# Sparse attention and mixture of experts: the scores of a unit in four 64x64 quarters of the array

## The chip, the cores and the metric

One Trainium2 chip, one of its cores. The metric is the device time of one execution in microseconds, taken as the median of several runs; the profile shown is of one further execution. The engines are PE (TensorE, the 128x128 matmul array), DVE (VectorE), ACT (ScalarE), POOL (GpSimd) and SP, which here only issues DMAs.

## The reference

Attention over 8 batches, 8 heads, 576 positions and head width 64, all fp32. The first four heads see a local window, the last four a strided pattern; then every position goes through its best two of eight experts.

```
rel = pos[:, None] - pos[None, :]
mask_local = (rel >= 0) & (rel < 32)
mask_strided = (rel >= 0) & (pos[None, :] % 32 == pos[:, None] % 32)
scores = where(mask, q @ k.T / 8, -1e9);  attn = softmax(scores);  x = attn @ v
logits = x @ w_gate;  noisy = logits + log1p(exp(x @ w_noise)) * noise
top2 experts e of each row, weights softmaxed over the two
out = sum of weight_e * (relu(x @ w1[e]) @ w2[e])
```

Here x has 4608 rows of 512; w1 is 512x1024 and w2 1024x512 for each expert.

## The kernel before, in words

The program has two stages that overlap a little: attention with the routing of each batch, and then the experts.

**Units.** Attention runs over 32 units. A unit is one batch and two heads, either two local or two strided ones, in turn. Its queries are cut into 9 blocks of 64. A local block needs 96 keys (its own 64 and the 32 before), a strided block, whose positions are taken apart by their residue, 72. So a unit has 18 score products, each of 64 queries by 96 or 72 keys with 64 (the head width) summed over: each fills a quarter of the array, 64 rows by 64 columns.

**A unit's steps** (lines as in the profile): SP loads k, q and v (L403). `prep` brings k and q into transposed form kT and qT, head 0 on partitions 0 to 63 and head 1 on 64 to 127: eight of the nine blocks from whole-row tiles (L461, after a reordering copy `ord`, or L471), the ninth, which stands alone in small tiles `k0` and `q0` of 64 partitions, by two transposes (L489). `item` is then called twice a unit, for blocks 0 to 3 and for blocks 4 to 8. An item writes the masks into a PSUM bank with a bf16 product of `twin` (two 64x64 identities side by side, so a 64-row by 128-column product, L518) and adds the products of both heads (L525): head 0 lands on partitions 0 to 63, head 1 on 64 to 127 of the same bank, so the products alternate between the two quarters on the array's diagonal. DVE takes the row maxima of the bank (L536), ACT the exponentials, one instruction per block (L540), PE transposes them (L548), ACT or DVE copies them out as aT, PE multiplies by v (L571, and L577 for the ninth block), DVE divides by the sums (L582 to L595) into xo. `finish` stores xo to x_dram (L612) and transposes it into xT (L634, and L631 for the ninth block of 64 rows); for a strided unit the copy out of PSUM (L247 on ACT or L250 on DVE) also puts the positions back in order, writing every eighth element. After four units `route` runs the gate of a batch (L679), the noisy top two (L682 to L764), and POOL scatters entries into a table (L769).

**Experts.** A job gathers up to 384 rows of one expert (POOL, L905), transposes them (DVE, L930), and multiplies by w1 (L963) and w2 (L1027) in split fp32r products; rows of `out` are read, added to and scattered back. Four jobs use only the entries of the first half of the batches and may run while attention still does. Weights are loaded by SP (L834, L837) into `wraw` and split by ACT and DVE (L839, L840).

**The order.** Nothing in the loop over units sets the order of instructions. Each step is a `Piece` with an engine, a planned duration, a rank and what it reads and writes; `issue_all` lays them out in planned time, lowest rank among those that could start within 120 ns, and that is the order on each engine. Eight PSUM banks are handed out by it; attention keeps to 7 while an expert piece waits. The planner chooses ACT or DVE for copies. SP's DMAs and POOL's stand in one queue each, in planned order, and an instruction waits at the head of its queue.

## Time and profile before

| what | before |
|---|---|
| median of 3 runs (lowest, highest) | 1200.76 us (1199.69, 1200.79) |
| the profiled execution, its own time | 1190.76 us |
| its span, first to last instruction | 1189.0 us |
| mean granted TensorE clock | 0.956 |
| PE / DVE / ACT / POOL busy | 95% / 51% / 33% / 52% |
| last gate of attention starts (L679) | 326.59 us |
| first expert product (L963) | 259.8 us |

The profiled execution took 10.0 us less than the median of the runs. All times inside the program are from it. "PE busy" counts a matmul until its modelled end, so back-to-back small products look busy to the last; the steps from one group's start to the next group's start tell more. The granted clock goes between full speed and half of it. An fp32 product leaves two records on PE, so 8 products are written x16; a transpose leaves one.

### The profile page before, as it was taken

Reading aid. Unit: us, or ns where it says so; the run is one execution under the profiler, and the core shown is the slowest. Engines: PE = TensorE matmul, PEld = TensorE weight load, DVE = VectorE, ACT = ScalarE, POOL = GpSimd, SP = SyncE. Lnnn points to the kernel's source line nnn. Section 1 sums busy time; section 2 is a strip of 40 time slices with the busy share of each in tenths; the row PEclk is TensorE's granted clock in tenths of the full one; section 3 lists DMA queues with packets and bytes.
Section 4 is the critical chain, followed back from the end, with each engine's and each line's share of the span. In section 5 each row is a group of like instructions: output and inputs, shape, how many; then the busy total and the mean of one; then the engine's idle time right before and its main releaser. Section 6 shows DMA issues by size and latency. Waiting matters only on the chain.

```text
span 1189.0 us, 23202 instructions
## 1 busy us (share of the span) xinstructions
...
## 2 busy tenths in 40 slices
...
GB/s 172 173 141 175 195 180 160 138 154 162 231 247 195 231 128 70 134 155 70 131 149 97 140 130 125 159 71 64 146 138 79 78 191 80 75 119 116 83 47 20
DMA packets 211941, 159.01 MB, mean 134 GB/s; under 512 B 90967, under 2 KB 181591, under 8 KB 211808
## 3 DMA queue, kind: packets, MB, share of 16 engines
...
q14 instruction: 53, 0.43, 0.1%
...
## 4 chain that ended last, share of the span: by engine, by line
PE 87%; DMA 4%; DVE 3%; issue 3%; ACT 2%; SPq 0%; another core or an unknown queue 0%; POOL 0%; POOLq 0%; DVEq 0%; ACTq 0%
PE bankA L1027 5%; PE bankG L963 4%; PE bankD L1027 4%; PE bankD L963 4%; PE bankF L1027 4%; PE bankE L963 4%; PE bankC L1027 4%; PE bankG L1027 4%; PE bankB L963 4%; PE bankA L963 4%; PE bankH L963 4%; PE bankC L963 4%; PE bankF L963 4%; PE bankH L1027 4%; PE bankE L1027 4%; PE bankB L1027 3%
## 5 line engine op out<-in xcount | busy, mean ns | idle before, releaser
L905 POOL DMA_INDIRECT xg<-x_dram,gxx x304 | 315.7, 1038 | 180.6 <-issue 76.5
L769 POOL DMA_INDIRECT tab<-ent,addr x96 | 91.7, 955 | 121.0 <-DVE mx L536 24.2
L1057 POOL DMA_INDIRECT out_dram<-prev,tabt x80 | 85.6, 1071 | 94.8 <-issue 38.9
L1004 POOL DMA_INDIRECT prev<-out_dram,gix x80 | 79.6, 995 | 66.4 <-issue 28.6
L930 DVE STREAM_TRANSPOSE xr<-xg 128x512 f32<-128x512 f32 x80 | 84.3, 1054 | 31.5 <-DMA xg<-x_dram,gxx 25.0
L934 ACT CAST xhi<-xr 128x512 fp32r<-128x512 f32 x80 | 47.9, 598 | 86.3 <-DVE xr L930 78.7
L839 ACT CAST w2hi<-wraw 128x512 fp32r<-128x512 f32 x88 | 51.6, 617 | 44.9 <-DMA wraw<-in_moe_w_dram 26.7
L840 DVE TENSOR_TENSOR w1lo<-wraw,w1hi 128x512 fp32r<-128x512 f32 x88 | 60.3, 688 | 11.4 <-ACT w1hi L839 6.3
L936 DVE TENSOR_TENSOR xlo<-xr,xhi 128x512 fp32r<-128x512 f32 x80 | 53.2, 665 | 25.0 <-ACT xhi L934 22.0
L840 DVE TENSOR_TENSOR w2lo<-wraw,w2hi 128x512 fp32r<-128x512 f32 x88 | 57.6, 684 | 5.5 <-ACT w2hi L839 4.0
L839 ACT CAST w1hi<-wraw 128x512 fp32r<-128x512 f32 x88 | 54.2, 618 | 17.6 <-DMA wraw<-in_moe_w_dram 17.3
L982 ACT ACTIVATE hhi<-bankE 128x256 fp32r<-128x256 f32 (+2 forms) x33 | 14.0, 424 | 105.1 <-PE bankE L963 81.8
L963 PE MATMUL bankE<-xhi,w1lo 128*128 128x256 f32 (+3 forms) x132 | 40.0, 303 | 0.4 <-issue 0.4
L963 PE MATMUL bankC<-xhi,w1hi 128*128 128x256 f32 (+3 forms) x128 | 38.3, 299 | 1.9 <-ACT w1hi L839 1.9
L963 PE MATMUL bankE<-xhi,w1hi 128*128 128x256 f32 (+3 forms) x132 | 40.0, 303 | 0.0
L982 ACT ACTIVATE hhi<-bankH 128x256 fp32r<-128x256 f32 (+2 forms) x32 | 13.6, 425 | 79.0 <-PE bankH L963 73.0
L963 PE MATMUL bankD<-xhi,w1hi 128*128 128x256 f32 (+3 forms) x132 | 39.9, 302 | 0.0
L963 PE MATMUL bankD<-xlo,w1hi 128*128 128x256 f32 (+3 forms) x132 | 39.4, 298 | 0.4 <-issue 0.4
L963 PE MATMUL bankE<-xlo,w1hi 128*128 128x256 f32 (+3 forms) x132 | 39.7, 301 | 0.0
L963 PE MATMUL bankD<-xhi,w1lo 128*128 128x256 f32 (+3 forms) x132 | 39.6, 300 | 0.0
L963 PE MATMUL bankG<-xhi,w1hi 128*128 128x256 f32 (+3 forms) x132 | 39.6, 300 | 0.0
L963 PE MATMUL bankG<-xhi,w1lo 128*128 128x256 f32 (+3 forms) x132 | 39.3, 298 | 0.0
...
## 6 DMA issues: line engine op xcount, KB each, us to landing
...
```

What stands on the lines that cost most here:

```text
L769: st = nc.gpsimd.indirect_dma_start(out=tab, out_offset=bass.IndirectOffsetOnAxis(ap=s["addr"].t[:, t, kk:kk + 1], axis=0), in_=s["ent"].t ...
L839: Piece("ACT", act(512) + 30, lambda o: nc.scalar.copy(hi.t, raw.t), rank, read=[raw], alloc=[hi], expert=True)
L840: Piece("DVE", dve(512), lambda o: nc.vector.tensor_tensor(lo.t, raw.t, hi.t.bitcast(F32), ALU.subtract), rank, read=[raw, hi], alloc=[lo] ...
L905: dma(lambda o, i=i, g=g, xg=xg: nc.gpsimd.indirect_dma_start(out=xg.t[:, g, :], out_offset=None, in_=x_dram[:4 * known, :], in_offset=bas ...
L930: Piece("DVE", dve(4 * rows), lambda o, xg=xg, xr=xr, ng=ng, rows=rows: nc.vector.transpose(xr.t[:, :, :rows].rearrange("p c (g i) -> p g ...
L934: Piece("ACT", act(4 * rows), lambda o, xr=xr, rows=rows, cols=cols: nc.scalar.copy(xh.t[:, :, cols], xr.t[:, :, :rows]), rank, read=[xr], ...
L936: Piece("DVE", dve(4 * rows), lambda o, xr=xr, rows=rows, cols=cols: nc.vector.tensor_tensor(xl.t[:, :, cols], xr.t[:, :, :rows], xh.t[:, ...
L963: nc.tensor.matmul(ps.t[:, :width], a.t[:, 128 * d:128 * d + 128], c.t[:, d, :width], start=(m == 0), stop=(m == len(todo) - 1))
L982: Piece("ACT", act(width) + 30, lambda o: nc.scalar.activation(hh.t[:, :width], ps.t[:, :width], AF.Relu), rank, read=[ps], alloc=[hh], ex ...
L1004: dma(lambda o: nc.gpsimd.indirect_dma_start(out=pv.t[:rows, :], out_offset=None, in_=out[:known, :], in_offset=bass.IndirectOffsetOnAxis( ...
L1027: nc.tensor.matmul(ps.t, HT[n, f][p[0]].t[:, cols], W2[n][f][p[1]].t, start=(m == 0), stop=(m == len(todo) - 1))
L1057: st = nc.gpsimd.indirect_dma_start(out=out[:known, :], out_offset=bass.IndirectOffsetOnAxis(ap=tb.t[:rows, i, 0:1], axis=0), in_=pv.t[:ro ...
```

## The change

- `products` replaces the scores of both items: a unit's masks and all 18 products are one piece on PE that takes two banks at once. Bank b belongs to head b, partitions 0 to 63 of it to the even blocks, 64 to 127 to the odd ones; the ninth block of head b stands as a fifth column group on half b. Masks are written by 64x64 products into all four quarters (`twin` and the masks stand on both halves of the partitions for that). The order of the 16 first products goes round the four quarters; the ninth blocks follow as a pair.
- An item is now one head, with both banks' ninth blocks in item 1. The row maximum is taken over five column groups in both items; the exponentials of the ninth block are two instructions of 64 partitions, one from each bank.
- `kq0` holds the ninth block's k on partitions 0 to 63 and its q on 64 to 127 (two DMAs as before), and one 128x128 transpose takes the place of two.
- `finish` transposes the ninth block as full 128 rows (xo's lower half is zero there). For strided units the four transposes write PSUM with a step of eight, so that the copy to xT is contiguous; the stores of x go out in rows of 256 elements where they were of 128. v_0 has 72 partitions, the last 8 zero.
- At the start DVE makes two copies of masks and five more memsets.

```diff
-    twin = consts.tile([QB, 2, QB], BF16, name="twin")
-    for h in range(2):
-        nc.vector.tensor_copy(twin[:, h, :], ident[:QB, :QB])
...
+    halves = [slice(QB * h, QB * h + QB) for h in range(2)]
+    twin = consts.tile([2 * QB, QB], BF16, name="twin")
+    for r in halves:
+        nc.vector.tensor_copy(twin[r, :], ident[r, r])
...
+            if o.psums:
+                n = len(o.psums)
                 if o.expert and left_a and held[0] >= expert_banks:
                     return None
-                if not free or not o.expert and e == "PE" and filler[0] and len(BANKS) - len(free) - held[0] >= ATT_BANKS:
+                if len(free) < n or not o.expert and e == "PE" and filler[0] and (
+                        len(BANKS) - len(free) - held[0] + n - 1 >= ATT_BANKS):
                     return None
-                t = max(t, min(free.values()) + 220)
+                t = max(t, sorted(free.values())[n - 1] + 220)
...
-            ("k0", [QB, 2, D], F32, 2), ("q0", [QB, 2, D], F32, 2),
+            ("kq0", [2 * QB, 2, D], F32, 2),
...
+        put("kq0", R["kq0"].new(),
+            [(lambda t, r=r: t[r], src, base + (512 * D if local else 0), [[D, QB], [S * D, 2], [1, D]], 65536)
+             for r, src in zip(halves, (k, q))], True)
...
             ps = Slot()
-            ks, qs = L["k0"], L["q0"]
-            def tr(o):
-                for i, s in enumerate((ks, qs)):
-                    nc.tensor.transpose(ps.t[:, QB * i:QB * i + QB], s.t, ident[:QB, :QB])
-            Piece("PE", 120, tr, rank, read=[ks, qs], psum=ps)
+            kq = L["kq0"]
+            Piece("PE", 115, lambda o: nc.tensor.transpose(ps.t[:, :2 * QB], kq.t, ident), rank, read=[kq], psum=ps)
...
-    def item(u, i, kT, qT, L, xo, rank):
+    def products(u, kT, qT, rank):
...
+        local = units[u][2]
+        w = KW if local else G
+        sc = [Slot(), Slot()]
+        def scores(o):
+            sv = [s.t[:, :5 * w].rearrange("r (n c) -> r n c", n=5) for s in sc]
+            for half in range(2):
+                for b, r in enumerate(halves):
+                    if local:
+                        spans = [(0, 5, mask_l2[r, 1:2, :])] if half else [(0, 1, mask_l2[r, 0:1, :]),
+                                                                           (1, 5, mask_l2[r, 1:2, :])]
+                    else:
+                        spans = [(0, 4, mask_s2[r, 0:1, :]), (4, 5, mask_s2[r, 1:2, :])]
+                    for n0, n1, mk in spans:
+                        nc.tensor.matmul(sv[b][halves[half], n0:n1, :], twin[r, :], mk.to_broadcast([QB, n1 - n0, w]),
+                                         start=(n0 == 0), stop=False, skip_group_check=True)
+            def product(b, s, half, blk):
+                r = halves[b]
+                rhs = kT.t[r, QB * blk:QB * blk + KW] if local else kT.t[r, blk, :]
+                nc.tensor.matmul(sv[b][halves[half], s, :], qT.t[r, blk, :], rhs, start=False,
+                                 stop=True, skip_group_check=True)
+            for s in range(4):
+                for half in range(2):
+                    for b in range(2):
+                        product(b, s, half, 2 * s + half)
+            for b in range(2):
+                product(b, 4, b, NBL - 1)
+        o = Piece("PE", 20 + 10 * w / 4.8 + 5 * (188 if local else 144), scores, rank, read=[kT, qT], psum=sc)
+        o.order += in_turn[-1:]
+        in_turn.append(o)
+        return sc
...
-        sc, mx, ex = Slot(), R["mx"].new(), R["ex"].new()
+        sc, mx, ex = scs[i], R["mx"].new(), R["ex"].new()
         aT, rs = R["aT"].new(), R["rs"].new()
-        def scores(o):
-            sv = sc.t[:, :nb * w].rearrange("r (n c) -> r n c", n=nb)
-            if local:
-                spans = [(0, nb, mask_l[:, 1:2, :])] if i else [(0, 1, mask_l[:, 0:1, :]), (1, nb, mask_l[:, 1:2, :])]
-            else:
-                spans = [(0, 4, mask_s[:, 0:1, :])] + ([(4, nb, mask_s[:, 1:2, :])] if i else [])
-            for n0, n1, mk in spans:
-                nc.tensor.matmul(sv[:, n0:n1, :], twin.rearrange("p h x -> p (h x)"),
-                                 mk.to_broadcast([QB, n1 - n0, w]), start=(n0 == 0), stop=False, skip_group_check=True)
-            for n in range(nb):
-                blk = 4 * i + n
-                rhs = kT.t[:, QB * blk:QB * blk + KW] if local else kT.t[:, blk, :]
-                for h in range(2):
-                    r = slice(64 * h, 64 * h + 64)
-                    nc.tensor.matmul(sv[r, n, :], qT.t[r, blk, :], rhs[r], start=False, stop=True,
-                                     skip_group_check=True)
-        o = Piece("PE", 110 + nb * w / 2.4 + (188 if local else 144) * nb, scores, rank, read=[kT, qT], psum=sc)
-        o.order += in_turn[-1:]
-        in_turn.append(o)
...
-        Piece("DVE", dve(nb * w), lambda o: nc.vector.tensor_reduce(mx.t[:, :nb], view(sc), AX.X, ALU.max, negate=True),
+        Piece("DVE", dve(5 * w), lambda o: nc.vector.tensor_reduce(mx.t, view(sc), AX.X, ALU.max, negate=True),
               rank, read=[sc], alloc=[mx])
         def exps(o):
-            for n in range(nb):
+            for n in range(4):
                 nc.scalar.activation(exv()[:, n, :], view(sc)[:, n, :], AF.Exp, bias=mx.t[:, n:n + 1])
-        Piece("ACT", nb * (act(w) + 82), exps, rank, read=[sc, mx], alloc=[ex])
+            for r, s, m in zip(halves, scs, mxs) if i else ():
+                nc.scalar.activation(exv()[r, 4, :], view(s)[r, 4, :], AF.Exp, bias=m.t[r, 4:5])
+        Piece("ACT", (4 + 2 * i) * (act(w) + 82), exps, rank, read=[*scs, *mxs] if i else [sc, mx], alloc=[ex])
...
         def scaled(o):
-            dst = xo.t[:, 2 * i:2 * i + 2, :, :].rearrange("r g h d -> r (g h) d") if local else xo.t[:, :4, i, :]
-            nc.vector.tensor_tensor(dst, main()[:, :, :D], rs.t[:, :4, None].to_broadcast([128, 4, D]), ALU.mult)
-            if i:
+            if local:
+                nc.vector.tensor_tensor(xo.t[:, :4, i, :], main()[:, :, :D], rs.t[:, :4, None].to_broadcast([128, 4, D]),
+                                        ALU.mult)
+            else:
+                nc.vector.tensor_tensor(
+                    xo.t[:, i:4:2, :, :].rearrange("r m h d -> r h m d"),
+                    main()[:, :, :D].rearrange("r (h m) d -> r h m d", h=2),
+                    rs.t[:, :4].rearrange("r (h m) -> r h m", h=2)[:, :, :, None].to_broadcast([128, 2, 2, D]), ALU.mult)
+            if nb > 4:
                 nc.vector.tensor_tensor(xo.t[:QB, 4, :, :], extra()[:, :, :D],
                                         rs.t[:QB, 4:, None].to_broadcast([QB, 2, D]), ALU.mult)
-        Piece("DVE", 80 * (1 + i), sums, rank, read=[po], alloc=[rs])
-        Piece("DVE", 95 * (1 + i), recip, rank, write=[rs], read=[rs])
-        Piece("DVE", dve(256) + i * dve(128), scaled, rank, read=[po, rs],
+        Piece("DVE", 80 * (nb - 3), sums, rank, read=[po], alloc=[rs])
+        Piece("DVE", 95 * (nb - 3), recip, rank, write=[rs], read=[rs])
+        Piece("DVE", dve(256) + (nb - 4) * dve(128), scaled, rank, read=[po, rs],
...
         else:
             for half in range(2):
-                store(lambda t, half=half: t[64 * half:64 * half + 64, :4, :, :].rearrange("r g h d -> r g (h d)"),
-                      (QB + half) * 128, [[NJ * 128, QB], [2 * 128, 4], [1, 128]], 131072)
+                store(lambda t, half=half: t[64 * half:64 * half + 64, :4, :, :].rearrange(
+                    "r (m g) h d -> r m (g h d)", m=2),
+                      (QB + 2 * half) * 128, [[NJ * 128, QB], [4 * 128, 2], [1, 256]], 131072)
             store(lambda t: t[:QB, 4, :, :].rearrange("r h d -> r (h d)"), 0, [[128, QB], [1, 128]], 32768)
...
             def tr(o, c=c, ps=ps):
                 if c:
-                    nc.tensor.transpose(ps.t[:, :QB], xo.t[:QB, 4, :, :], ident[:QB, :QB])
+                    nc.tensor.transpose(ps.t[:, :128], xo.t[:, 4, :, :], ident)
                 else:
+                    pv = ps.t.rearrange("r (x m h g) -> r m g h x", m=2, h=2, g=2)
                     for g in range(4):
-                        nc.tensor.transpose(ps.t[:, 128 * g:128 * g + 128], xo.t[:, g, :, :], ident)
-            Piece("PE", 60 if c else 430, tr, rank, read=[xo], psum=ps)
+                        nc.tensor.transpose(ps.t[:, 128 * g:128 * g + 128] if local else pv[:, g // 2, g % 2, :, :],
+                                            xo.t[:, g, :, :], ident)
+            Piece("PE", 110 if c else 430, tr, rank, read=[xo], psum=ps)
             def dst(c=c):
                 if local:
                     return xt.t[:, 512:] if c else xt.t[:, :512]
-                return xt.t[:, :QB] if c else xt.t[:, QB:].rearrange("r (x j) -> r j x", j=NJ)
+                return xt.t[:, :QB] if c else xt.t[:, QB:]
             def src(ps=ps, c=c):
                 if c:
                     return ps.t[:, :QB]
-                return ps.t if local else ps.t.rearrange("r (j x) -> r j x", j=NJ)
+                return ps.t
             Piece("ANY", {"ACT": act(n), "DVE": dve(n)}, lambda o, dst=dst, src=src: copy(o.e, dst(), src()), rank,
```

**Where it moves instructions.** PE, the scores of the first local unit, before (twin is the pair of identities, kT_l and qT_l the transposed k and q):

```order
L518 LDWEIGHTS twin
L518 MATMUL bankE<-mask_l,twin 128x96
L518 LDWEIGHTS twin
L518 MATMUL bankE<-mask_l,twin 128x288
L525 MATMUL bankE<-kT_l,qT_l 64x96 x8
L518 LDWEIGHTS twin
L518 MATMUL bankC<-mask_l,twin 128x480
L525 MATMUL bankC<-kT_l,qT_l 64x96 x10
```

and in the changed kernel, with the same products in turn on two banks:

```order
L532 MATMUL bankG<-mask_l,twin 64x96
...
L532 MATMUL bankG<-mask_l,twin 64x384
...
L532 MATMUL bankA<-mask_l,twin 64x96
...
L532 MATMUL bankA<-mask_l,twin 64x384
...
L532 MATMUL bankG<-mask_l,twin 64x480
...
L532 MATMUL bankA<-mask_l,twin 64x480
L538 MATMUL bankG<-kT_l,qT_l 64x96
L538 MATMUL bankA<-kT_l,qT_l 64x96
```

Three mask products a unit became six (three became eight in a strided unit), and one piece stands where two stood with other work between them.

SP, the first loads, before:

```order
L403 DMA ks<-in_k_dram 72x2x512
L403 DMA k_185<-in_k_dram 64x2x64
L403 DMA qs<-in_q_dram 72x2x512
L403 DMA q_189<-in_q_dram 64x2x64
L403 DMA v_s_123<-in_v_dram 72x8x64
```

and now:

```order
L417 DMA ks<-in_k_dram 72x2x512
L417 DMA qs<-in_q_dram 72x2x512
L417 DMA kq_197<-in_k_dram 64x2x64
L417 DMA v_s_125<-in_v_dram 72x8x64
L417 DMA v_127<-in_v_dram 64x2x64
L417 DMA kq_197<-in_q_dram 64x2x64
```

The number of loads is the same; the second half of the small tile moved behind a load of v.

PE, around the last gate (L679, now L716), before. 96 products of layer 1 and 12 of layer 2 of the experts stand ahead of that gate; L1027 is layer 2, L686 and L730 belong to the routing of the last batch:

```order
L1027 MATMUL bankG<-w2hi,hlo 128x512
L679 MATMUL bankC<-xT,wg 32x192 x12
L1027 MATMUL bankD<-w2hi,hhi 128x512
...
L686 MATMUL bankE<-ident,lgT 96x96 x2
L1027 MATMUL bankG<-w2hi,hhi 128x512
...
L730 MATMUL bankH<-ohs,upper 96x48
```

and now, with 96 and 42 ahead of it (L1064 is layer 2, L1000 layer 1, L723 and L767 the routing):

```order
L716 MATMUL bankB<-xT,wg 32x192 x12
L1064 MATMUL bankG<-w2hi,hhi 128x512
...
L723 MATMUL bankA<-ident,lgT 96x96 x2
L1000 MATMUL bankE<-xhi,w1hi 128x256
...
L767 MATMUL bankH<-ohs,upper 96x48
```

So 30 products of layer 2 moved ahead of the last gate; between the gate and L767 stand 6 products of layer 2 and 24 of the next job's layer 1, where 12 of layer 2 stood.

81 lines of the change are left out of this document (41 added, 40 removed).

## The prediction

> **What bounds the kernel now.** I read the chain of waits first, then the span cut into three stretches, then PE step by step. Chain by engine, and the stretches (length, then busy us and instructions of PE, weight loads, DVE, ACT and POOL, then granted clock, DMA share, GB/s):
>
> ```profile
> PE 87%; DMA 4%; DVE 3%; issue 3%; ACT 2%; SPq 0%; another core or an unknown queue 0%; POOL 0%; POOLq 0%; DVEq 0%; ACTq 0%
> 0.00:327.00 327.00, 299.33 (x3665) 234.27 (x3668) 192.74 (x786) 162.45 (x549) 118.12 (x241) 0.88 0.74 171
> 327.00:430.00 103.00, 93.86 (x542) 79.86 (x537) 67.29 (x141) 44.18 (x91) 65.47 (x78) 0.95 0.76 220
> 430.00:1189.00 759.00, 739.48 (x4251) 663.68 (x4249) 348.75 (x615) 189.00 (x403) 431.86 (x464) 0.99 0.36 106
> ```
>
> The change touches the first stretch, attention: PE is busy 299 of 327 us there, DVE 193, ACT 162, so PE's steps come first. Two things dilute them. The DMA engines are at 0.74 on the mean, and the clock at 0.88 means about 78 us at half speed (0.12 x 327 / 0.5). Three short stretches show both (same columns):
>
> ```profile
> 66.00:68.00 2.00, 0.64 (x5) 0.43 (x3) 0.69 (x1) 1.35 (x6) 1.00 (x2) 0.50 0.94 223
> 70.00:80.00 10.00, 10.00 (x88) 7.44 (x86) 4.18 (x14) 1.88 (x6) 3.01 (x6) 0.50 0.66 138
> 130.00:140.00 10.00, 9.55 (x143) 7.60 (x141) 7.61 (x49) 7.28 (x24) 1.88 (x5) 1.00 0.95 229
> ```
>
> From 70 to 80 PE never rests and still goes at half speed. From 130 on the DMA engines are full; of the 33 ten-us stretches to 330 eight have a share of 0.90 or more.
>
> **The scores, now.** PE at full clock (start, busy us, line, operation, count; the step is the time to the next row's start):
>
> ```profile
> 42.20 0.27 PE L489 MATMUL bankD<-ident,k 64*128 64x64 f32 x1
> ...
> 42.47 0.66 PE L461 MATMUL bankB<-ident,ord 128*128 128x128 f32 x4
> 43.05 0.69 PE L571 MATMUL bankH<-v_l,aT 96*64 96x65 f32 x16
> ...
> 43.90 0.29 PE L518 MATMUL bankG<-mask_s,twin 64*128 64x288 bf16 x1
> 44.12 0.72 PE L525 MATMUL bankG<-kT_s,qT_s 64*64 64x72 f32 x16
> 44.77 0.33 PE L518 MATMUL bankC<-mask_s,twin 64*128 64x288 bf16 x2
> 45.03 0.84 PE L525 MATMUL bankC<-kT_s,qT_s 64*64 64x72 f32 x20
> 45.80 0.66 PE L634 MATMUL bankA<-ident,xo 128*128 128x128 f32 x4
> 46.39 0.27 PE L631 MATMUL bankF<-ident,xo 64*128 64x64 f32 x1
> 46.59 0.65 PE L461 MATMUL bankE<-ident,ord 128*128 128x128 f32 x4
> 47.08 0.60 PE L548 MATMUL bankB<-ident,ex 128*72 128x128 f32 x4
> 47.61 1.50 PE L679 MATMUL bankH<-xT,wg 128*32 128x192 f32 x24
> 49.04 0.69 PE L571 MATMUL bankG<-v_s,aT 72*64 72x65 f32 x16
> ...
> 50.31 0.27 PE L548 MATMUL bankE<-ident,ex 128*72 128x128 f32 x1
> 50.51 0.34 PE L518 MATMUL bankC<-mask_l,twin 64*128 64x96 bf16 x2
> 50.78 0.88 PE L525 MATMUL bankC<-kT_l,qT_l 64*64 64x96 f32 x16
> 51.59 0.69 PE L571 MATMUL bankD<-v_s,aT 72*64 72x65 f32 x16
> ...
> 52.58 0.37 PE L518 MATMUL bankB<-mask_l,twin 64*128 64x480 bf16 x1
> 52.88 1.04 PE L525 MATMUL bankB<-kT_l,qT_l 64*64 64x96 f32 x20
> 53.85 0.53 PE L548 MATMUL bankH<-ident,ex 128*96 128x128 f32 x3
> ```
>
> Strided: masks 0.22 + 0.26, products 0.65 + 0.77, together 1.90 a unit. Local: masks 0.27 + 0.30, products 0.81 + 0.97, together 2.35. Ten products take 0.16 more than eight (local) and 0.12 (strided): that is one pair on the diagonal, and 0.81 - 4 x 0.16 leaves 0.17 fixed a group. The 288-column mask (0.22) and the 480-column one (0.30) give 0.10 fixed and 0.42 ns a column.
>
> **The scores, after.** If four quarters go at once, 18 products are four steps of four and one pair: local 5 x 0.16 + 0.17 = 0.97 for 1.78, strided 5 x 0.12 + 0.17 = 0.77 for 1.42. No row has 64x64 products in four quarters. The nearest that share the array are the three column tiles of L679: 24 records of 192 columns in 1.43 us, 0.31 ns a column, where the diagonal pair takes 0.16 / (4 x 96) = 0.42. So three at a time get further than two. At L679's rate a step of four would take 0.24 and 0.18, and the sum below would be 15 instead of 24; I take full overlap, because three tiles already reach nine tenths of their share (0.28 by the pair's rate).
>
> The masks lose the shared write of both halves. If all quarters overlap they cost what one long mask does (0.30 and 0.26), if none 4 x 0.20 + 0.10 = 0.90 and 4 x 0.15 + 0.10 = 0.70. They start in program order. In a strided unit the 72-column mask waits for the 288-column one of its own quarter, and the next quarter's waits behind it: 4 x 0.12 + 0.03 + 0.10 = 0.61. A local unit puts the short mask first, so the last long one starts about 0.10 after the first: 0.40. I take these.
>
> Per unit: local -0.81 - 0.17 = -0.98, strided -0.65 + 0.13 = -0.52; times 16 each, **-24.0 us** at full clock. Ends: all overlaps, -1.08 and -0.87, 31 us less; only diagonals overlap, as now, and masks not at all: -0.17 + 0.33 and -0.17 + 0.22 (one fixed part fewer), 3.4 us more.
>
> **The other PE edits.** Two transposes of k and q (L489, 0.27) become one like the single L548 (0.20): 32 x -0.07 = -2.2. The ninth block's finish goes from 0.20 (L631) to that same 0.20: 0. The four strided transposes of finish will write PSUM with a step of eight elements. L461 already writes with a step of four, in 0.58 and 0.49, where L634 writes contiguously in 0.59: I take 0. PE sum: **-26 us**.
>
> **ACT, DVE, SP.** (start, busy, line, forms; a tile's copies with lowest, median and highest ns; waits at SP's head with total, times, longest.)
>
> ```profile
> 64.19 0.96 ACT L540 ACTIVATE ex<-bankC,mx 128x72 f32<-128x72 f32 x4 [4.37 <-DVE mx L536]
> 65.11 1.21 ACT L540 ACTIVATE ex<-bankA,mx 128x72 f32<-128x72 f32 x5
> 63.65 0.44 DVE L536 TENSOR_REDUCE mx<-bankC 128x4 f32<-128x288 f32 x1
> 64.02 0.52 DVE L536 TENSOR_REDUCE mx<-bankA 128x5 f32<-128x360 f32 x1
> L250 DVE COPY xT<-bankG x4: 1084/1090/1103, 39.4 to 275.7; 128x512 f32<-128x512 f32 x4
> L250 DVE COPY xT<-bankA x4: 194/686/694, 46.5 to 324.9; 128x512 f32<-128x512 f32 x3, 128x64 f32<-128x64 f32 x1
> 6.57 0.46 DVE L250 COPY kT_s<-bankB 128x288 f32<-128x288 f32 x1 [2.61 <-PE bankB L471]
> L612 SPq DMA_DIRECT2D x_dram<-xo x80: 377/570/3094, 21.7 to 323.8; - x80
> SPq L612 <- DVE xo L595: 24.4, 11, 6.7
> ```
>
> One more exponential a unit, 0.25 x 32 = +8.0; a longer maximum, 0.08 x 32 = +2.6; 16 copies of xT at 1.09 become contiguous ones at 0.69, -6.4. That is +4.2 over two engines with 130 and 160 us free: 0, and 4 if none of it were covered. The new DVE work at the start (two mask copies, five memsets, about 1 us) lies in DVE's idle 2.61 before 6.57; uncovered, 1. On SP half of the small k/q tile moved behind two loads of v: at about 0.57 an issue its transpose is 1.1 late in the first unit. Later units load ahead, and the transpose is the last of its unit's: 0, ends 0 and 1.1 a unit, 35. Stores get half as many, longer rows, the same bytes: 0, with 2 us of gain as the other end.
>
> The new wait: a head's maximum now stands behind all 18 products. DVE's queue holds the copies behind it, and ACT's exponentials wait for it as at 64.19 (4.37). It comes about 0.5 later for the first item and sooner for the second; values follow 4.9 us after scores (44.12 to 49.04), which covers it. That the scores want two free banks at once has no row; ends are 0 and one exponential group (1.0) a unit, 32. The plan starts scores where two are free, so I take 0 for it and let the next part hold the rest.
>
> **How much reaches the end.** Not all 26. A quarter of the stage (8 of 33 stretches) has full DMA engines, where PE only waits longer. In about another quarter SP's loads queue behind stores that wait for a unit's end (24.4 us, eleven times, up to 6.7; that they hold a quarter is my estimate). Ends none and all; I take half, **13 us**. Of it 7.0 appear as expert work: 30 products of layer 2 now ahead of the last gate, at 0.233 (six from 339.06 to 340.46). The gate itself comes about 6 earlier, 320.6. Behind it:
>
> ```profile
> ACT w1hi L839 <- DMA wraw<-in_moe_w_dram: 15.4, 13, 3.3
> 334.17 0.22 PE L730 MATMUL bankH<-ohs,upper 96*96 96x48 bf16 x1 [2.88 <-DVE oh L715]
> 339.06 0.40 PE L1027 MATMUL bankD<-w2hi,hhi 128*128 128x512 f32 x1
> ...
> 340.46 0.40 PE L1027 MATMUL bankG<-w2hi,hhi 128*128 128x512 f32 x1
> ```
>
> ACT waits here for weights that come when they come, 1.2 us a time. The fillers after the gate are now layer-1 products of the next job and need them. Two such waits more, 2.5 us, are lost (ends: -2.9, the gap before L730 filled, and 15). 13 - 2.5 = 10.5: the profiled execution's 1190.76 becomes 1180.3. It ran 10.0 below the median, so 1200.76 becomes **1190.3**; with a third or two thirds of the 26 instead of half, 1184 to 1197 after rounding outward.
>
> **Rivals.** *All of it arrives* (0.17): PE 299 of 327 busy speaks for it, the full DMA stretches against. 26 less 2: 1177. *The loads set the stage* (0.12): DMA 0.74 and SP's waits speak for it, that PE is 87% of the chain against. PE's gain becomes waiting: 1200. *Slower by the clock* (0.10): denser scores leave PE lighter between units, and more spells run at half speed. For it: about 78 us run so now, and at 66 to 68 such a spell holds a PE that works 0.64 of 2.00; against it, 70 to 80, where full work stays slow. Each us more at half clock costs half of one, so it decides from 21 us more; with half as much again, 39, it costs 20 against 10.5: 1210. [...] *Writes with a step of eight slow the transposes* (0.03): if the 16 groups double, 16 x 0.59 = 9.4 comes back, the PE sum is 17, half of it less 2.5 is 6: 1195. The step grows from four to eight; that L461 is not slowed by four speaks against. [...] *Quarters on the same rows take turns* (0.03): the change then doesn't do what it says, and PE has 3.4 - 2.2 more: 1202.
>
> **How the numbers follow.** Forecast 0.55, rivals as given. I call 0.2% (2.4 us) what a measurement can tell from no change. Faster: 0.55 + 0.17 + 0.03 = 0.75. Within: the loads' case 0.12 and two thirds of the last, 0.14. Slower: the clock and the rest, 0.11. The range from 1176 to 1204 takes in the forecast, the first two rivals and the last; the clock's case (0.10) is left out, and as much again for the tails of the others.
>
> **What would show it.** Each unit's scores, masks first to next group, at 1.4 local and 1.4 strided at full clock (2.4 and 1.9 if quarters take turns); xT copies all near 0.69; finish's strided transposes at 0.59, not 1.2; the last gate near 320 with 42 products of layer 2 ahead; half-clock time near 78 us; DMA share of attention up to about 0.76. A gate at 327 with PE less busy would mean the loads; half-clock time over 100, the clock; ACT waiting over 5 us more for weights, that the gain was given back after the gate.

## The result: faster, by three times the forecast

| | before | changed |
|---|---|---|
| median of 4 runs (lowest, highest), us | 1200.22 (1197.92, 1200.79) | 1165.51 (1158.95, 1166.78) |
| ratio, 95% interval | | 0.971 (0.967 to 0.974) |
| profiled execution, its span | 1190.76, 1189.0 | 1158.95, 1157.1 |
| last gate starts | 326.6 | 300.7 |
| from there to the end of the span | 862.4 | 856.4 |

The forecast was 1190.3 with a range down to 1176; the change gained 34.7 us and lies below the range. In the profiled executions the spans differ by 31.9: 25.9 ahead of the last gate, although 30 more products of layer 2 (7.0 us) stand ahead of it, and 6.0 behind it. One slow execution of the change in e7_after_again took 4219 us and is left out of the median given for that run below.

The span of the changed kernel in three stretches (columns as in the prediction), with the cut at the gate:

```profile
0.00:303.00 303.00, 257.07 (x3806) 207.91 (x3806) 195.07 (x796) 170.15 (x594) 123.35 (x242) 0.92 0.82 191
303.00:400.00 97.00, 88.02 (x509) 77.85 (x509) 61.93 (x134) 41.54 (x86) 65.44 (x80) 0.93 0.75 217
400.00:1157.00 757.00, 736.97 (x4234) 660.36 (x4232) 346.47 (x613) 188.17 (x401) 421.67 (x463) 0.99 0.35 106
```

PE is busy 257 us of attention where it was 299, and idle 46 where it was 28. The clock is 0.92 instead of 0.88, about 50 us at half speed instead of 78. DMA share went from 0.74 to 0.82: much the same bytes (by the GB/s 56 and 58 MB) in less time.

PE's steps in the changed kernel, at full clock: a strided unit's scores (L532 masks, L538 products), what follows them, and a local unit's scores.

```profile
39.46 0.31 PE L532 MATMUL bankG<-mask_s,twin 64*64 64x288 bf16 x1
39.47 0.31 PE L532 MATMUL bankB<-mask_s,twin 64*64 64x288 bf16 x1
...
39.60 0.19 PE L532 MATMUL bankG<-mask_s,twin 64*64 64x72 bf16 x1
...
39.64 0.25 PE L538 MATMUL bankG<-kT_s,qT_s 64*64 64x72 f32 x1
...
40.40 0.69 PE L598 MATMUL bankD<-v_l,aT 96*64 96x65 f32 x16
...
41.73 0.27 PE L500 MATMUL bankF<-ident,kq 128*128 128x128 f32 x1
41.84 0.60 PE L579 MATMUL bankA<-ident,ex 128*72 128x128 f32 x4
...
54.00 0.23 PE L532 MATMUL bankA<-mask_l,twin 64*64 64x96 bf16 x1
...
54.01 0.39 PE L532 MATMUL bankA<-mask_l,twin 64*64 64x480 bf16 x1
...
54.06 0.32 PE L532 MATMUL bankA<-mask_l,twin 64*64 64x384 bf16 x1
...
54.23 0.24 PE L538 MATMUL bankA<-kT_l,qT_l 64*64 64x96 f32 x1
...
55.16 0.37 PE L723 MATMUL bankE<-ident,lgT 96*96 96x96 f32 x2
55.46 0.69 PE L598 MATMUL bankD<-v_s,aT 72*64 72x65 f32 x16
55.97 0.40 PE L603 MATMUL bankD<-v,aT 72*64 72x65 f32 x4
56.30 0.47 PE L485 MATMUL bankC<-ident,qs 72*128 72x72 f32 x4
```

| step at full clock, us | before | forecast | measured |
|---|---|---|---|
| local: masks, products | 0.57, 1.78 | 0.40, 0.97 | 0.23, 0.93 |
| strided: masks, products | 0.48, 1.42 | 0.61, 0.77 | 0.18, 0.76 |
| ninth blocks of k and q | 0.27 | 0.20 | 0.11 |
| strided values, second item | 0.99 | (not seen) | 0.84 |

The order of the starts is the news: all four 288-column masks start within 0.02 us, and the 72-column ones from 39.60 on, though in the program each stands right behind the 288-column mask of its own quarter and ahead of the next quarter's. In the local unit a 480-column mask starts at 54.01 and the 384-column ones, which stand ahead of it, at 54.06.

Sums: scores 16 x (1.19 + 0.96) = 34.4, ninth transposes 32 x 0.16 = 5.1, strided values 16 x 0.15 = 2.4, together 41.9 us less of PE at full clock, where 26 were forecast. The budget up to the gate: 41.9 less of PE and some 9 from 28 us less at half clock (the 9 is a difference, not a measurement), less 18 more of idle PE, is the 25.9 and the 7.0.

Two corrections to the description. In a strided unit partitions 0 to 63 and 64 to 127 of kT and qT hold the even and odd positions, not the two heads (the ninth block alone is by head). An item of the changed kernel is therefore one head in a local unit and one parity in a strided one; no number hangs on that. And the change also brings a new rule of the planner, which the description leaves out and the forecast doesn't name:

```diff
             for s in write:
                 self.order.append(s.writers[0])
+
+                for x in read:
+                    if s.ring is not None and x.ring is None and x not in s.writers[0].touch:
+                        x.writers[0].order.append(s.writers[0])
```

A piece that fills a PSUM bank for a tile already begun is now planned no earlier than the first copy into that tile. It stands in all versions of the change, in e1_rest, g2_rest and h2_ninth below, and not in h1_xt.

### The profile page after: what moved, and what is told of

The parts are those of the page before. It is cut to its first block, busy times and chain, and to the rows that moved or that the text cites. A ratio compares the mean times of both kernels' runs of the same rounds, so it can differ in the third digit from the quotient of the medians.

```text
span 1157.1 us, 23398 instructions
## 1 busy us (share of the span) xinstructions
PE 1082.1 (94%) x8546; PEld 946.1 (82%) x8546; DVE 603.5 (52%) x1542; ACT 399.9 (35%) x1081; POOL 610.5 (53%) x783
## 4 chain that ended last, share of the span: by engine, by line
PE 85%; issue 3%; DMA 3%; DVE 3%; ACT 2%; another core or an unknown queue 0%; SPq 0%; POOL 0%; POOLq 0%; DVEq 0%; ACTq 0%
PE bankH L1064 5%; PE bankA L1064 5%; PE bankB L1000 5%; PE bankF L1000 5%; PE bankB L1064 4%; PE bankF L1064 4%; PE bankA L1000 4%; PE bankE L1000 4%; PE bankG L1000 4%; PE bankD L1000 4%; PE bankC L1000 4%; PE bankH L1000 4%; PE bankC L1064 4%; PE bankE L1064 4%; PE bankD L1064 4%; PE bankG L1064 4%
## 5 line engine op out<-in xcount | busy, mean ns | idle before, releaser
L942 POOL DMA_INDIRECT xg<-x_dram,gxx x304 | 308.5, 1015 | 180.1 <-issue 85.5
L806 POOL DMA_INDIRECT tab<-ent,addr x96 | 94.5, 985 | 95.4 <-issue 14.8
L1019 ACT ACTIVATE hhi<-bankD 128x256 fp32r<-128x256 f32 (+2 forms) x31 | 13.2, 426 | 88.6 <-PE bankD L1000 65.0
L1000 PE MATMUL bankB<-xhi,w1hi 128*128 128x256 f32 (+3 forms) x132 | 40.2, 305 | 1.5 <-ACT hhi L1019 1.3
L1000 PE MATMUL bankE<-xhi,w1hi 128*128 128x256 f32 (+3 forms) x136 | 41.2, 303 | 0.3 <-issue 0.3
L1000 PE MATMUL bankB<-xhi,w1lo 128*128 128x256 f32 (+3 forms) x132 | 40.1, 304 | 0.8 <-issue 0.7
L1000 PE MATMUL bankE<-xhi,w1lo 128*128 128x256 f32 (+3 forms) x136 | 40.5, 298 | 0.0
L1000 PE MATMUL bankF<-xhi,w1lo 128*128 128x256 f32 (+3 forms) x128 | 39.1, 305 | 1.5 <-DVE w1lo L877 1.5
L1000 PE MATMUL bankE<-xlo,w1hi 128*128 128x256 f32 (+3 forms) x136 | 40.2, 296 | 0.0
L1000 PE MATMUL bankB<-xlo,w1hi 128*128 128x256 f32 (+3 forms) x132 | 39.7, 301 | 0.4 <-issue 0.4
L1000 PE MATMUL bankC<-xhi,w1hi 128*128 128x256 f32 (+3 forms) x132 | 39.4, 299 | 0.0
L1000 PE MATMUL bankF<-xhi,w1hi 128*128 128x256 f32 (+3 forms) x128 | 39.1, 305 | 0.3 <-issue 0.3
L1000 PE MATMUL bankC<-xhi,w1lo 128*128 128x256 f32 (+3 forms) x132 | 39.3, 298 | 0.0
```

Source lines behind the costliest of these rows:

```text
L806: st = nc.gpsimd.indirect_dma_start(out=tab, out_offset=bass.IndirectOffsetOnAxis(ap=s["addr"].t[:, t, kk:kk + 1], axis=0), in_=s["ent"].t ...
L942: dma(lambda o, i=i, g=g, xg=xg: nc.gpsimd.indirect_dma_start(out=xg.t[:, g, :], out_offset=None, in_=x_dram[:4 * known, :], in_offset=bas ...
L1000: nc.tensor.matmul(ps.t[:, :width], a.t[:, 128 * d:128 * d + 128], c.t[:, d, :width], start=(m == 0), stop=(m == len(todo) - 1))
L1019: Piece("ACT", act(width) + 30, lambda o: nc.scalar.activation(hh.t[:, :width], ps.t[:, :width], AF.Relu), rank, read=[ps], alloc=[hh], ex ...
```

## The experiments

All ratios are to the kernel before, timed in turn on the same chip. The change is called "the change", and "us" in a comparison is worked out from medians.

| run | what | ratio (95% interval) | kernel before on that chip |
|---|---|---|---|
| e6_before_again | before | 0.999 (0.995 to 1.003) | 1159.5 |
| e7_after_again | change | 0.986 (0.977 to 0.995) | 1159.5 |
| f1_after | change | 0.988 (0.983 to 0.992) | 1161.3 |
| e8_after | change | 0.972 (0.968 to 0.977) | 1200.7 |
| e3_by_quarter | change, products by quarter | 0.998 (0.994 to 1.002) | 1160.0 |
| f2_by_quarter | the same | 0.995 (0.992 to 0.998) | 1161.3 |
| g1_by_quarter | the same | 0.985 (0.980 to 0.991) | 1195.0 |
| e4_twice | change, scores twice | 0.998 (0.995 to 1.002) | 1160.0 |
| f3_twice | the same | 0.994 (0.991 to 0.997) | 1161.3 |
| e1_rest | all but the quarters | 0.994 (0.990 to 0.997) | 1160.0 |
| g2_rest | the same | 0.984 (0.979 to 0.989) | 1195.0 |
| h1_xt | contiguous xT alone | 0.999 (0.996 to 1.003) | 1199.1 |
| h2_ninth | ninth-block edits, planner's new rule | 0.982 (0.977 to 0.987) | 1199.1 |
| e5_old_cost | change, old plan costs | 0.999 (0.994 to 1.003) | 1160.0 |
| e9_fill | change, PE filled | 0.975 (0.969 to 0.981) | 1200.7 |
| e10_no_v | change, few loads of v | 0.973 (0.967 to 0.979) | 1200.7 |
| e11_store_act | change, stores by ACT | 0.992 (0.989 to 0.995) | 1200.7 |
| f4_two_ks | change, two k tiles | 0.987 (0.983 to 0.991) | 1161.3 |

### Two kinds of chips

The first four runs were meant to split the change into its parts.

e1_rest is the kernel before with everything but the quarters and what hangs on them (an item per head, the longer rows of the stores):

```diff
-            ("k0", [QB, 2, D], F32, 2), ("q0", [QB, 2, D], F32, 2),
+            ("kq0", [2 * QB, 2, D], F32, 2),
...
-                    kw = w if local else QB
-                    nc.tensor.matmul(extra()[:, h, :], aT.t[:kw, 4, 64 * h:64 * h + 64], rhs, start=True, stop=True)
+                    nc.tensor.matmul(extra()[:, h, :], aT.t[:w, 4, 64 * h:64 * h + 64], rhs, start=True, stop=True)
...
-                    nc.tensor.transpose(ps.t[:, :QB], xo.t[:QB, 4, :, :], ident[:QB, :QB])
+                    nc.tensor.transpose(ps.t[:, :128], xo.t[:, 4, :, :], ident)
...
-                        nc.tensor.transpose(ps.t[:, 128 * g:128 * g + 128], xo.t[:, g, :, :], ident)
+                        nc.tensor.transpose(ps.t[:, 128 * g:128 * g + 128] if local else pv[:, g, :, :],
+                                            xo.t[:, g, :, :], ident)
```

> The kernel before with every part of the change except the four quarters: one transpose for the ninth blocks of k and q, ninth value products over 72 rows, full-row finish, contiguous copies of xT. Theory A (the quarters carry nearly all of the 35 us, the rest only its 5 to 7 us of PE steps): 1193 to 1198. Rival B (the rest carries a good part, because copies, stores and fewer switches of row count free other engines too): 1185 or less.

Measured: 1152.3, and the kernel before beside it took 1160.0 at the median of 31, not 1200. So the times that these first expectations name can't be compared; ratios can, and by its ratio of 0.994 the run lies in theory A's bounds (0.993 to 0.998). Two runs asked whether this was the chip:

> The kernel before, unchanged, as a run of its own with a profile, on the chip of this call. In the runs so far on another chip the kernel before took 1160 at the median of 31, where it had taken 1200 when the change was timed. Theory A (chips differ in the pace of loads or in the clock, and where attention is not held back by PE the change has less to give): the time is again well under 1200, the ratio to the kernel before is 1.00 by construction, and the trace shows a last gate some 25 us earlier than 326.6 with less half-clock time or higher GB/s. Rival B (the 1160 came from something in that one call): 1195 to 1202 with the last gate at 327.

> The changed kernel, unchanged, on the same chip as the run of the kernel before. Theory A (the gain depends on the chip's state: where the kernel before takes 1160, the change gains 0 to 10): 1150 to 1160, ratio 0.99 to 1.00. Rival B (the change gains its 3% everywhere, and the four kernels of the last call were all slowed by what they undo): ratio 0.97, 1125 beside 1160 or 1165 beside 1200.

Before 1161.2 and change 1146.9, on another chip again; a third gave 1161.3 and 1147.0, a fourth 1200.7 and 1167.0:

> The changed kernel on the chip of this call, the base for the three other runs here. So far two kinds of chips were met: the kernel before took 1200 and the change 1165 to 1167 on the one, 1160 and 1148 on the other. Theory A: one of these two pairs again. Rival B: a ratio of 0.97 also where the kernel before takes 1160, which would make the run with 1148 a stray.

> The changed kernel once more, beside the kernel before on one chip, to place the earlier runs. Theory (the gain is set by how much half-clock time the kernel before meets on the chip of the day: per batch of four units the traces so far give 33.6 us plus 0.54 for each us at half clock before, 30.7 plus 0.58 after): with 1160 before, 1146 to 1152, ratio 0.988 to 0.994; with 1200 before, 1160 to 1167. Rival (the gain is the same 3% on every chip): ratio 0.968 to 0.974.

The last gate of the kernel before came at 308.1 in e6, 18.5 earlier than in the first profile, with 58 instead of 78 us at half speed before it. That is theory A of e6, with a smaller shift than its 25. The change's 0.986 in e7 is just outside A's 0.99 to 1.00 (its interval reaches 0.995), f1 repeats one of the two known pairs, and the same 3% on every chip is out (f1: 0.983 to 0.992). The times of e8 and f1 fall within e8's theory, 1167.0 at its very edge; that half-speed time sets the gain, as that theory has it, isn't shown by this.

So there are two kinds of chips for this kernel. On the one (call it the 1200 kind: the first timing and three chips of the experiments) the change gains 34 to 35 us, on the other (the 1160 kind, three chips) 13 to 14.

What tells the kinds apart in the trace is not the length of any common instruction (their medians agree within 2% in e8 and f1) and not the transfers (591 and 588 us of work for each DMA engine there), but the waits that the profile puts down to "issue", in which an engine waits for nothing that is seen. In the dense part (430 to 1130 us) of the change on a chip of the 1200 kind, groups by waiting instruction (total us, times, longest):

```profile
POOL xg L942 <- issue: 68.6, 180, 3.8
DVE hlo L1024 <- issue: 38.8, 31, 3.1
ACT hhi L1019 <- issue: 26.9, 19, 7.1
```

and of the same kernel on a chip of the 1160 kind, where DVE and ACT have no such row:

```profile
POOL xg L942 <- issue: 46.5, 140, 4.5
POOL out_dram L1094 <- issue: 28.0, 31, 14.0
```

In attention (0 to 300 us) PE has 36 such waits (14.0 us in all) on the first and none on the second. Over all runs the DVE row parts the kinds (39 us and more against 2 and less), while PE's waits do so less cleanly (5.4 us and more against 6.8 and less). The clock differs as well: the kernel before was granted 0.955 at the median on two chips of the 1200 kind (about 108 us at half speed) and 0.969 on the 1160 kind (72 us), while the change was granted 0.960 and 0.958, nearly the same. Why a chip is of one kind was not tried.

### The quarters

Undone by order alone: the 18 products go quarter after quarter, all other instructions stay.

```diff
-            for s in range(4):
-                for half in range(2):
-                    for b in range(2):
-                        product(b, s, half, 2 * s + half)
-            for b in range(2):
-                product(b, 4, b, NBL - 1)
+            for b in range(2):
+                for half in range(2):
+                    for s in range(4):
+                        product(b, s, half, 2 * s + half)
+                    if b == half:
+                        product(b, 4, b, NBL - 1)
```

> The changed kernel with the 18 products of a unit written quarter after quarter (4 or 5 in a row into the same quarter) instead of in turn; everything else in the same order. The trace of the change shows masks of a later quarter starting before the second mask of an earlier one. Theory A (each quarter has its own line of waiting products, and order in the program matters little): 1164 to 1170, score steps of about 1.2 local and 0.95 strided. Rival B (PE starts products in program order, so only the ends of quarters overlap): a local unit's products take up to 18 x 0.16 = 2.9 instead of 0.9, 2.0 more, strided 1.5 more, 56 us of PE in all, and two thirds of that at the end: 1195 to 1210.

PE by steps, a local unit of f2_by_quarter:

```profile
54.62 0.23 PE L532 MATMUL bankA<-mask_l,twin 64*64 64x96 bf16 x1
...
54.85 1.12 PE L538 MATMUL bankA<-kT_l,qT_l 64*64 64x96 f32 x15
55.74 0.29 PE L538 MATMUL bankH<-kT_l,qT_l 64*64 64x96 f32 x1
55.82 0.24 PE L538 MATMUL bankA<-kT_l,qT_l 64*64 64x96 f32 x1
55.87 0.24 PE L538 MATMUL bankH<-kT_l,qT_l 64*64 64x96 f32 x1
55.90 0.24 PE L538 MATMUL bankA<-kT_l,qT_l 64*64 64x96 f32 x1
55.96 0.24 PE L538 MATMUL bankH<-kT_l,qT_l 64*64 64x96 f32 x1
55.98 0.24 PE L538 MATMUL bankA<-kT_l,qT_l 64*64 64x96 f32 x1
56.04 1.12 PE L538 MATMUL bankH<-kT_l,qT_l 64*64 64x96 f32 x15
57.09 0.37 PE L723 MATMUL bankE<-ident,lgT 96*96 96x96 f32 x2
```

The unit takes 2.47, in rival B's direction though less, with the masks as quick as ever (0.23). A quarter alone takes 0.16 a product, and the next quarter does wait while several products of the one ahead stand in a row. The rows show how long: the first product into bankH starts at 55.74, when three records into bankA (55.82, 55.90, 55.98) have yet to start; a product is two records. It is three at this place in all 79 units of the three runs by quarter that ran at full clock without a break. The masks fit that: when the last 288-column mask starts, three 72-column ones that stand ahead of it are still waiting. So three blocked records were passed in both cases. The step went up by 1.31 local and, at 1.97, by 1.03 strided: 37.4 us of PE. And yet the time moved little on this chip; hence the repeat beside the change on one chip, with a second way to add PE work:

> The changed kernel with products written quarter after quarter, which by its trace costs 2.47 instead of 1.16 a local unit and 1.97 instead of 0.94 a strided one: 16 x 2.34 = 37 us more of PE steps at full clock, nothing else changed, now on the same chip as the change. Theory A (about 0.6 of PE's steps reach the end): +18 to +28 against the change. Theory B (waits for other engines and loads set the stage): under +8. Theory C (all of it counts): +34 or more.

The other way computes masks and products twice:

```diff
-        o = Piece("PE", 20 + 10 * w / 4.8 + 5 * (188 if local else 144), scores, rank, read=[kT, qT], psum=sc)
+        o = Piece("PE", 20 + 10 * w / 4.8 + 5 * (188 if local else 144), lambda o: (scores(o), scores(o))[1], rank, read=[kT, qT], psum=sc)
```

> The changed kernel with masks and products of every unit computed twice in a row, the second time over the first; same order on all engines. It adds 16 x (1.16 + 0.94) = 34 us of PE steps at full clock. Theory A (PE sets the pace of attention, about two thirds of its work counts): +20 to +30, 1186 to 1196. Rival B (loads set the pace and the gain came from elsewhere): under +8, below 1174. Rival C (PE counts in full, and slower score steps bring back half-clock time): +34 or more, 1200 and above.

> The changed kernel with masks and products computed twice, by its trace 2.19 instead of 1.16 local and 1.75 instead of 0.94 strided: 16 x 1.84 = 29 us more of PE steps, on the same chip as the change. It differs from the run by quarters in that the array is in full use meanwhile. Theory A (0.6 of PE's steps, the clock follows use of the array, and half-clock time comes out lower than by quarters): +8 to +18, and at least 5 less than by quarters. Theory B (only steps count): four fifths of what the run by quarters costs.

Change 1147.0, by quarter 1154.9, twice 1154.0: 37.4 us of PE cost 7.9, and 29 cost 7.0, on the 1160 kind, each within some 5 us by the scatter of the runs. (On the chip of e3 and e4 the change itself wasn't timed; if it has its 0.986 to 0.988 there, their 0.998 means some 12 to 14.) Where the rest of the 37.4 stays is seen in attention up to the gate, which starts at 294.25 in the change and 302.68 by quarter; first row the change (f1_after), second by quarter:

```profile
0.00:294.00 294.00, 247.50 (x3782) 204.55 (x3782) 194.75 (x795) 170.53 (x594) 124.03 (x242) 0.88 0.83 194
0.00:303.00 303.00, 280.71 (x3788) 241.02 (x3791) 201.18 (x796) 172.09 (x594) 124.02 (x242) 0.92 0.81 189
```

PE is idle 46.5 us in the change and 22.3 by quarter: 24 of the 37 that the change saves only turned into waiting. And the clock is 0.88 against 0.92, about 70 us at half speed against 48: here the PE with less to do was granted less clock, worth about 5 by difference. What is left, 8.4, is the gate. Theories A and C of f2 are out, and B (under 8) is met at its edge. For f3, A is out; whether 7.0 is B's four fifths of 7.9 is beyond the scatter. A's part on the clock holds weakly: 0.972 granted at the median for the scores done twice, 0.9685 by quarter, 0.9575 for the change.

On the 1200 kind:

> The run by quarters once more (37 us more of PE steps than the change, all else the same), for a chip of the kind where the kernel before takes 1200 and the change 1166. On the other kind it cost 8 us. Theory A (there the saved PE steps reach the end, because the same chips show waits of all engines for their own instructions, and these lie on the path together with PE): 1186 to 1205, 20 us or more over the change. Theory B (the difference between the kinds of chips lies outside the scores): 1170 to 1178. On a chip where the kernel before takes 1160: 1153 to 1160, as before.

1178.65 beside 1195.0: 0.985, where the change has 0.972 and 0.971 on that kind. The quarters are worth 1.3%, some 15 us of their 37 (7 to 24 by the intervals), compared through the kernel before across chips; that is between theory A and theory B. Attention up to the gate, which starts at 322.8, 18 later than in e8_after:

```profile
0.00:323.00 323.00, 293.04 (x3788) 250.32 (x3791) 197.50 (x795) 172.09 (x594) 123.03 (x242) 0.90 0.76 177
```

PE is idle 30 us here and 45 in e8, so less of the work hides in waits than on the 1160 kind. The clock is 0.90 in both: in these two traces the busier PE was not granted more (0.965 against 0.9605 at the median of the runs).

### The rest

> The kernel before with all parts of the change but the quarters, for a chip of the kind where the kernel before takes 1200. On the other kind it gained 8 us of the 13. Theory A (quarters carry most of the gain where it is 34): 1185 to 1196. Theory B (the rest carries most of it, as on the other kind): 1180 or less. On a chip where the kernel before takes 1160: 1149 to 1156.

1172.9 beside 1195.0: the rest alone gives 1.6% (1.1 to 2.1) on the 1200 kind, 0.6% (0.3 to 1.0) on the 1160 kind. By quarter, the other way to take the quarters out, gave 0.985 and 0.995, so the two agree. The rest carries about half of the gain, against the forecast's 2.2 of 26; g2's time is in theory B's bounds. Its two parts were timed apart: h1_xt has only finish's strided writes and the contiguous copies, h2_ninth only the one transpose of k and q, value products over 72 rows and the full-row finish (the first three pieces of the diff above), and with them the planner's new rule, which h1_xt doesn't have.

> The kernel before with one part of the rest alone: finish's strided transposes write PSUM with a step, so that the 16 copies of xT are contiguous (1.09 to about 0.69 us each on DVE or ACT; no PE step changes). The whole rest gave 22 us where the kernel before took 1195 and 8 us where it took 1160. Theory A (DVE and ACT lie on the chain from scores to the end of a unit, so shorter copies count): a third to two thirds of the rest, 7 to 14 us or 3 to 5 us by the kind of chip. Theory B (the copies are hidden, as the prediction had it): within 2.4 us.

> The kernel before with the other part of the rest alone: one transpose for the ninth blocks of k and q, ninth value products over 72 rows, full-row finish of the ninth block. By steps in the traces 0.15 us less a unit for the transpose and 0.15 less a strided unit for the values, 7.3 us of PE in all, with no more work elsewhere. Theory A (PE steps count by half or more): 4 to 8 us less than before on either kind of chip. Theory B (the order that the plan makes of new durations moves more than the steps): outside that, on either side.

The copies did become short (two banks' groups of h1_xt, ns lowest, median, highest), and the time didn't move:

```profile
L250 DVE COPY xT<-bankG x4: 691/692/693, 39.7 to 282.3; 128x512 f32<-128x512 f32 x4
L250 DVE COPY xT<-bankD x4: 677/686/692, 93.1 to 305.6; 128x512 f32<-128x512 f32 x4
```

They were hidden, as forecast (0.996 to 1.003). The ninth-block edits with the planner's rule give 1.8% (1.3 to 2.3), about 19 us, where the PE steps are 7.5 us shorter. Theory A's 4 to 8 fell, and theory B's "outside that" is met. Two further differences are known. The plan for h2_ninth puts 36 products of layer 2 ahead of the last gate instead of 12 (24 x 0.233 = 5.6 us of expert work done in waits). And its granted clock was 0.9645 at the median against 0.955 for the kernel before on the same chip, some 24 us less at half speed; among the runs of one kernel a us at half speed goes with 0.2 to 0.4 of time in most cases, so 5 to 10. Together with the steps that is enough for 19, but the three were not taken apart, no run has the edits without the rule or the rule without the edits, and that new plan and clock are the cause stays argued, not shown.

### What holds attention after the change

With PE idle 46 of 300 us, four runs looked for the next limit.

```diff
                 def tr(o):
+                    for _ in range(4 if (which, c) == ("k", 0) else 0):
+                        nc.tensor.matmul(ps.t.rearrange("r (a x) -> r a x", a=2), warm[:, :128],
+                                         warm[:, None, :].to_broadcast([128, 2, 256]), start=True, stop=True)
```

> The changed kernel with four bf16 products of 128x128 by 512 columns, of zeros, put ahead of the first transposes of k of every strided unit, where PE waits for a load (about 0.85 us each time at full clock, 14 us in all). They are free where PE waits there anyway. Theory A (half-clock time costs about half of itself, and is brought on by PE's light load at such waits): half-clock time of attention falls by 20 us or more, and the time by 0 to 8 us. Theory B (loads set the floor, the clock follows other things): half-clock time stays within 10 us, time 0 to +5. Rival C (PE's work counts in full): +14.

Attention of e9_fill, and of the change on the same chip:

```profile
0.00:304.00 304.00, 260.73 (x3846) 207.75 (x3846) 195.07 (x796) 170.86 (x594) 122.76 (x241) 0.95 0.82 188
0.00:304.00 304.00, 258.67 (x3780) 210.16 (x3781) 193.65 (x794) 169.31 (x592) 122.29 (x241) 0.90 0.80 186
```

Half speed fell from about 60 to 30 us, as theory A says: here the clock rose with more work on PE (0.971 against 0.9605 at the median of the runs). The time did not fall with it: the last gates start at 304.2 and 304.8, and the medians are 1168.2 and 1167.0. That the filling took what the clock gave is the likely reading.

```diff
-            put("v", slot, parts, True)
+            put("v", slot, parts if u < 4 else parts[:1], True)
...
-                 for h in range(2)], True)
+                 for h in range(2)] if u < 4 else
+                [(lambda t: t[:, 0, :1, :D], v, base, [[NJ * D, G], [D, 1], [1, D]], 18432)], True)
```

> The changed kernel without most loads of v: from the fifth unit on a unit loads only a first small piece of v and multiplies by the v of earlier units, so its output is not the reference's. It leaves out some 10 MB of the 36 MB that the units load. Theory A (after the change the loads set the floor of 30.7 us a batch): a batch falls to 27 us or less at full clock, 15 to 30 us less in all. Theory B (PE and the chain from load to store still set it): under 8 us less.

```profile
0.00:301.00 301.00, 260.84 (x3787) 212.79 (x3788) 197.81 (x809) 177.71 (x598) 122.18 (x240) 0.90 0.66 163
```

DMA share 0.66 instead of 0.80, and the same time (1168.0): the gate came 3.4 earlier than in e8, and the stretch behind it took 4.8 longer. The DMA engines' capacity isn't the limit on this kind; theory A fell.

```diff
-            stores[b].append(dma(lambda o: nc.sync.dma_start(dram(x_dram, base + off, dims), sel(xo.t)), nbytes, rank,
-                                 read=[xo]))
+            stores[b].append(Piece("ACT", 500, lambda o: nc.scalar.dma_start(dram(x_dram, base + off, dims), sel(xo.t)), rank,
+                                 read=[xo], lat=nbytes))
```

> The changed kernel with the stores of x issued by ACT's queue instead of SP's, so that loads no longer stand behind stores that wait for the end of a unit. Theory A (part of the floor is loads queued behind stores; SP waited about 20 us at the head of its queue for stores): 5 to 15 us less than the change. Theory B (the DMA engines are the floor): within 3 us. Rival C (ACT's exponentials now stand behind the stores' issue, 80 x 0.57): 10 us or more slower.

25 us slower than the change on that chip (1191.6), as rival C had it: an issue takes ACT 0.546 at the median, where it takes SP 0.558 in the profiled execution of the change (L644). The plan changed too (24 more products of layer 1 and 6 of layer 2 ahead of the gate), so not all of the 25 need be ACT's.

```profile
L644 ACTq DMA_DIRECT2D x_dram<-xo x80: 364/546/1944, 21.6 to 324.2; - x80
```

On the 1160 kind the largest waits of PE in attention are for the strided k. Rows of f1_after:

```profile
PE bankD L485 <- DMA ks<-in_k_dram: 8.9, 2, 7.1
PE bankF L485 <- DMA ks<-in_k_dram: 7.7, 2, 4.2
PE bankH L485 <- DMA ks<-in_k_dram: 6.1, 1, 6.1
```

A second tile for it:

```diff
-            ("ks", [G, 2, NJ, D], F32, 1), ("qs", [G, 2, NJ, D], F32, 1),
+            ("ks", [G, 2, NJ, D], F32, 2), ("qs", [G, 2, NJ, D], F32, 1),
...
-            ("xT", [128, S], F32, 6),
+            ("xT", [128, S], F32, 5),
```

> The changed kernel with two tiles for the strided k instead of one (and five for xT instead of six, for room), so that its load can be issued before the transposes of the unit before are done. In the change's traces PE's longest waits in attention are for this load, 9 to 36 us in all. Theory A (the load is late because its only tile is still in use): those waits fall below 5 us and the time by 5 to 15 us. Theory B (the load is late because of its place in SP's queue, or PE then waits for q instead): within 3 us of the change.

```profile
PE bankC L485 <- DMA qs<-in_q_dram: 11.9, 3, 4.6
PE bankF L485 <- DMA qs<-in_q_dram: 3.7, 1, 3.7
PE bankH L500 <- DMA kq<-in_q_dram: 3.7, 2, 1.9
```

The waits of PE for k fell from 30.5 to 1.1, and PE waits for q and the ninth blocks instead, as theory B says. The gate came 7.5 earlier (286.8), but from there to the end of the span took 855.7 instead of 850.4, with six products of layer 2 (1.4) fewer done ahead of the gate. 1146.1 against 1147.0: no difference. The waits for weights behind the gate grew, first row f1_after (294 to 400), second f4_two_ks (287 to 400):

```profile
ACT w2hi L876 <- DMA wraw<-in_moe_w_dram: 10.6, 9, 3.5
ACT w2hi L876 <- DMA wraw<-in_moe_w_dram: 14.4, 9, 4.0
```

No version here beat the change by more than the measurement.

### The order of the plan

```diff
-        o = Piece("PE", 20 + 10 * w / 4.8 + 5 * (188 if local else 144), scores,
+        o = Piece("PE", 220 + 9 * w / 2.4 + 9 * (188 if local else 144), scores,
```

> The changed kernel, but the plan is made with the old duration of a unit's scores; the products themselves run as in the change. The plan then puts 168 products of layer 1 and 48 of layer 2 ahead of the last gate instead of 96 and 42. Theory A (the gain is PE time, the order of the plan is second to it): within 5 us of the change, 1160 to 1171. Rival B (a good part of the gain came from the new order that the plan makes): half the gain or more is lost, 1183 or above.

1158.3, a ratio of 0.999, where the change has 0.988 and 0.986 on chips of that kind. The products are as fast as in the change; told the old cost, the planner laid 168 products of layer 1 into attention and put the gate at 317.4. About 11 us hang on the order here, nearly the whole gain on that kind of chip, compared across chips. In us the run lies inside theory A's bounds, which were set for the 1200 kind; by ratio it is rival B.

## Why the prediction was wrong

Two steps failed: the sum of PE's steps, 26 us where 41.9 was measured, above all by the masks; and the one share of a half for all of it, with the clock held near 78 us at half speed.

- **Bound and place** were right: the gain lies in attention, on PE.
- **Products** were right to 0.04 us: 0.97 and 0.77 forecast, 0.93 and 0.76 measured. Four quarters do overlap.
- **Masks** were the term of the sum that was mis-sized: "They start in program order", the author's assumption, failed: the 288-column masks of all four quarters start by 39.48, ahead of 72-column ones that wait until 39.60. 0.23 and 0.18 instead of 0.40 and 0.61 is 9.6 us more saved, below even the lower bound of 0.30 and 0.26, which had counted 0.10 fixed.
- **The ninth blocks**: "one like the single L548 (0.20)" was too dear, it measured 0.11, 2.9 more. That the strided value products get quicker with 72 rows in place of 64 (2.4) was overlooked: the quoted rows have 0.99 for them (51.59 to 52.58), the change 0.84 (55.46 to 56.30).
- **Writes with a step** were right: the four transposes of finish take 0.57 (126.54 to 127.11) in a strided unit, with the step of eight, and 0.49 (133.49 to 133.98) in the local unit after it, without. The rival's doubling to 1.18 was an assumption that no run shows; what follows the transposes differs, so the 0.08 between them is not put down to the step.

```profile
126.54 0.63 PE L670 MATMUL bankH<-ident,xo 128*128 128x128 f32 x4
127.11 0.57 PE L598 MATMUL bankD<-v_l,aT 96*64 96x65 f32 x12
...
133.49 0.66 PE L670 MATMUL bankD<-ident,xo 128*128 128x128 f32 x4 [0.89 <-DVE xo L619]
133.98 0.60 PE L579 MATMUL bankG<-ident,ex 128*72 128x128 f32 x4
```

- **ACT and DVE hidden** was right for the copies by h1_xt: 6.4 us less of them gave nothing (a ratio of 0.999). The added exponentials and maxima were not timed alone.
- **"How much reaches the end": half, everywhere.** This is the step that failed beside the sum. Of the quarters' 37 us (undone by order) some 8 reach the end on one kind of chip and some 15 on the other: less than half. With the ninth blocks' 7.5 came 19: more than twice. A share for all of PE's work doesn't exist here, since shorter steps also move the plan's order (e5_old_cost: 11 us) and the clock. The rival "All of it arrives" (1177) came nearest in time, but the runs by quarter rule its mechanism out.
- **The clock near 78 us** failed too. The clock's rival has its mechanism in one pair: a lighter PE was granted less clock in f1 than in f2 (about 70 us at half speed against 48). On the 1200 kind it went the other way, 78 to about 50 in the profiled executions, and helped. The rival's price of half a us for each was too high as well (0.2 to 0.4 in most cases among runs of one kernel). Why the kernel before runs so long at half speed on that kind was not found.
- **Loads as the limit**: that a quarter of the stage is bound by full DMA engines has e10_no_v against it on the 1200 kind, where leaving out most loads of v gave nothing (1168.0 against 1167.0). What bounds PE's waits there stays open.
- **Behind the gate**: 2.5 lost was forecast, 1.0 was (6.0 gained of the 7.0 moved ahead); waits for weights of the first such row went from 15.4 to 11.2. f4_two_ks shows the loss as forecast: an earlier gate is partly given back.

```profile
ACT w1hi L876 <- DMA wraw<-in_moe_w_dram: 11.2, 15, 3.2
```

The gain of 34.7 thus goes with a larger sum (41.9 for 26), a new order and less half-speed time; how much each of the three gave was not separated. By parts on that kind of chip: some 19 for the ninth blocks with the planner's rule, nothing for the copies, some 15 for the quarters. On a chip of the 1160 kind the forecast's 10.5 would have come near the 13 to 14 there, and that would have been luck: the sum was too small by 16 and the share too large.
